# Block-sparse attention and a swish-gated MLP on one core: batch 0 rebuilt with fewer matmuls and another order, and batch 1's values loaded ahead of the last quarter of w_out

## The chip, the cores and the metric

The kernel runs on one core of a Trainium2 chip. The metric is the device time of one execution in microseconds (us). The engines are TensorE (PE; its weight loads are listed apart as PEld), VectorE (DVE), ScalarE (ACT), GpSimd (POOL) and SyncE (SP). Each has a queue of its own that it works off in order. POOL and SP also issue the DMAs: POOL all loads from q, k, v and the weights, SP the copies inside the on-chip memory and the stores.

## What is computed

There are 4 batches, 8 heads, 768 tokens and 64 values per head. Each query sees the keys within 15 positions of its own, and beside them 24 summary keys (the maximum over each block of 32 keys, with log 32 added to the score); the summary values are means over the blocks. The attention's output, 3072 tokens of 512 values, goes through a two-layer MLP with a gate.

```python
mask_l = np.abs(pos[:, None] - pos[None, :]) < window          # window 16
scores_s = scale * np.einsum('bhsd,bhnd->bhsn', q, k_sum) + np.log(block)
scores_all = np.concatenate([np.where(mask_l, scores_l, -1e9), scores_s], axis=-1)
a = softmax(scores_all)
attn_out = a @ np.concatenate([v, v_sum], axis=2)
h = x @ w_in                                                    # 512 -> 2048
g = h * (1.0 / (1.0 + np.exp(-beta * h)))
out = g @ w_out                                                 # 2048 -> 512
```

## The kernel before, in words

The order on every engine is the order in which the program is written (`manual_schedule`); nothing is moved by a scheduler. Heads go in four pairs g = 0 to 3, with the two heads on partitions 0 to 63 and 64 to 127. Batch 0 is worked in an opening stage of its own, in halves `hf` of 384 tokens (3 chunks `m` of 128, each of two parts `par` of 64 queries). Batches 1 to 3 are worked as side work between the matmuls of the MLP (`h_group`, L482, for w_in; `o_part`, L503, for w_out), at places set by the numbers in the last loop (`at_time`).

The opening stage, in the order of the text from L534 on:

- `keep_warm`: eleven matmuls without use, while the first keys (`hold_k`, `hold_q`) arrive. `cast_hold` (L130, on DVE) turns these from f32 into bf16.
- `turn` (L271) transposes k or q of a pair on PE, per pair and tensor 16 matmuls of 64 columns: 8 slices `j` for each of two heads. `prep_k` copies the result to `kw` on ACT, `prep_q` to `qt` on DVE (pair 0: ACT), `top_k` (L285, DVE) takes the block maxima `km`.
- A loop over the pairs. `open_scores` (L354, L355) starts half 0 of a pair with the mask as a matmul: `identity` times `negband` (L354, one per head), and `identity` times `negedge` for the first 16 rows (L355, one per head). `scores_half` adds twelve score matmuls (L367) and two for the summary keys (L372), then Exp on ACT (L386). The loop's order on PE is: open half 0 of g, transpose k of g+1, half 0 of g, transpose q of g+1, half 1 of g. Half 1 of pair 3 is left for later. `band_edges` (DVE, three small instructions that finish the tile `band` for the second halves' mask) stands in the loop's first round.
- `copy_v` copies values to the other alignment (`vo`), half of it on DVE (L320) and half by DMA from SP. `mean_v` makes the block means (`vm_ps`, then `vm_first`, L332). `av_first` (L393 to L401) multiplies attention and values for a first half: one matmul by zeros over all 390 columns (L393), twelve for the near keys, six for the summary keys. `norm` (L446, L447, DVE) divides and gives `x_nat`; `x0` transposes it on PE (L461) and copies it to `xT`. The order is: means of pairs 0 and 1, av_first 0, norm, half 1 of pair 3, `load_beta` (a transpose on PE, L230, and two small DVE instructions, L231 and L232), av_first 1, norm, and so on to pair 3, with the first `h_group` matmuls between them.

POOL's queue is the third order that matters. The program issues, in this row: k and q of batch 0, its values (`load_v_edge`, `load_v`: `ve`, 384 KB per two pairs), w_in in five pieces, k and q of pairs 0 and 1 of batch 1, w_out in four pieces, values of batch 1 (edge and pairs 0 and 1), k and q of pairs 2 and 3, the other values, then batch 2. The framework gives these DMAs eight semaphores in turn, so an issue waits until the one eight places ahead of it has landed. From the landed values SP issues the copies `vo<-ve` of batch 1 (L320), whose landing `rows_v` (L341, DVE) and `av` (L437, PE) wait for.

Of the kernel before, what the change touches and what calls it, by code (L numbers as in the profile page):

```python
# [12 lines left out]
def kernel(  # L13
# [10 lines left out]
    nc = tc.nc  # L24
    ctx.enter_context(tc.manual_schedule(engines={getattr(mybir.EngineType, e) for e in ("SP", "Pool", "PE", "DVE", "Activation")}))
    P = 128
    f32 = mybir.dt.float32
    bf16 = mybir.dt.bfloat16
    ALU = mybir.AluOpType
    ACTF = mybir.ActivationFunctionType  # L30

    B, H, S, D = q.shape
    block = 32
    W = 16
    nb = S // block
    QT = 64
    nch = S // P
    NC = nch + 1
    J = 8
    PT = S // J  # L40
    npair = H // 2
    scale = 1.0 / math.sqrt(D)
# [5 lines left out]
    VW = D + 1  # L48
# [42 lines left out]
    def run_tile(nm, b, g):  # L91
        if (nm, b, g) not in nat:
            t = qk_pool.tile([PT, 4, J, D], bf16, name=nm + "_run", tag=nm + "_nat", bufs=2)
            for i in range(2):
                nat[(nm, b, g // 2 * 2 + i)] = t[:, 2 * i:2 * i + 2]
        return nat[(nm, b, g)]

    def load_run(nm, b, g, n=1):
        src = (k if nm == "k" else q)[b, 2 * g:2 * (g + n)].rearrange("h (p j) d -> p h (j d)", j=J)
        if n == 1:  # L100
            dst = run_tile(nm, b, g)
        else:
            dst = qk_pool.tile([PT, 4, J, D], bf16, name=nm + "_run", tag=nm + "_nat", bufs=2)
            for i in range(n):
                nat[(nm, b, g + i)] = dst[:, 2 * i:2 * i + 2]
        nc.gpsimd.dma_start(out=dst.rearrange("p h j d -> p h (j d)"), in_=src)  # L106
# [7 lines left out]
    def load_v(b, g, n=1):  # L114
        lo, hi = PC * g + 1, min(PC * (g + n) + 1, HC)
        rows = v[b].rearrange("h s d -> (h s) d")
        src = rows[lo * P - W:hi * P - W].rearrange("(c p) d -> p c d", p=P)
        nc.gpsimd.dma_start(out=ve_bufs[b % 2][:, lo:hi, 0:D], in_=src)  # L118
# [7 lines left out]
            nc.gpsimd.dma_start(out=ve[W:P, 0, 0:D], in_=rows[0:P - W])  # L126

    def cast_hold(nm, g, copy):
        f = hold.pop((nm, g))
        copy(out=run_tile(nm, 0, g).rearrange("p h j d -> p h (j d)"), in_=f[:])  # L130

    beta_tmp = wpool.tile([k2, P], f32, name="beta_tmp")
    beta_sb = wpool.tile([P, k2], f32, name="beta_sb")
# [9 lines left out]
    spare = const.tile([P, 1], f32, name="spare")  # L143
    near = const.tile([P, QT], bf16, name="near")
    band = const.tile([P, 2, nch, 2, QT], bf16, name="band")
    negband = const.tile([P, QT], bf16, name="negband")
    negedge = const.tile([P, QT], bf16, name="negedge")
    km_bufs = [const.tile([P, 32], bf16, name=f"km{i}") for i in range(npair)]
    vm_bufs = [const.tile([P, 2, VW], bf16, name=f"vm{i}") for i in range(2)]
    vm_first = const.tile([P, npair, 2, VW], bf16, name="vm_first")  # L150
# [1 line left out]
    def zero(t):  # L152
        nc.vector.memset(t, 0.0)
# [21 lines left out]
    nc.vector.memset(A_loc, 1.0)  # L175
    clear_k(0)
    clear_v(0)
    zero(negedge)
    nc.vector.memset(negedge[0:W], NEG)
    zero(A_avg)  # L180
    load_run("k", 0, 1)
    load_run("q", 0, 1)
# [27 lines left out]
    nc.scalar.copy(out=beta_sb[:, 0:1], in_=warm[:, 0:1])  # L210
    cast_hold("k", 0, nc.vector.tensor_copy)
    cast_hold("q", 0, nc.vector.tensor_copy)
    nc.scalar.activation(out=negband[:], in_=near[:], func=ACTF.Copy, scale=-NEG, bias=NEG)


    for par in range(2):
        nc.scalar.copy(out=band[:, par].rearrange("p m h f -> p (m h) f"), in_=near[:, None].to_broadcast([P, 2 * nch, QT]))

    def band_edges():
        zero(band[0:W, 0, 0])  # L220
        zero(band[D:SUM, 1, nch - 1])
        nc.vector.tensor_copy(out=band[D:D + W, 1, nch - 1], in_=near[D:D + W, None, :].to_broadcast([W, 2, QT]))
# [5 lines left out]
    def load_beta():  # L228
        beta_ps = psum([P, k2], f32, "beta_ps", "big")
        nc.tensor.transpose(beta_ps[:], beta_tmp[:], identity32[:k2, :k2])  # L230
        nc.vector.tensor_copy(out=beta_sb[:], in_=beta_ps[:])  # L231
        nc.vector.reciprocal(out=inv_beta[:], in_=beta_sb[:])  # L232
# [11 lines left out]
    def load_w_out(i, c=k2 // 4):  # L244
        nc.gpsimd.dma_start(out=w_out_sb[:, i * c:(i + 1) * c], in_=w_out_r[:, i * c:(i + 1) * c])
# [19 lines left out]
    def turn(nm, b, g, tag="t"):  # L265

        t = nat.pop((nm, b, g))
        p = psum([P, J, PT], bf16, "p" + nm, tag)
        for j in range(J):
            for h in range(2):  # L270
                nc.tensor.transpose(p[h * D:(h + 1) * D, j], t[:, h, j], identity[:PT, :PT])  # L271
        return p.rearrange("p j t -> p t j")
# [74 lines left out]
    def open_scores(g, hf):  # L347

        big = ps.tile([P, 2, 512], f32, name="s_ps", tag="big", bufs=3)
        s_open[(g, hf)] = big  # L350
        if hf == 0:
            for h in range(2):
                sv = big[:, h, 0:2 * HM * QT].rearrange("p (m r f) -> p m r f", r=2, f=QT)
                nc.tensor.matmul(sv, identity, negband[:, None, None, :].to_broadcast([P, HM, 2, QT]), start=True, stop=False)  # L354
                nc.tensor.matmul(sv[:, 0, 0], identity, negedge, start=False, stop=False)  # L355

    def scores_half(g, hf):
        if (g, hf) not in s_open:
# [29 lines left out]
    def av_first(g, tag):  # L388

        a = at.pop((0, g, 0))  # L390
        o = psum([P, 2 * HM * VW], f32, "av_ps", tag)
        ov = o.rearrange("p (h m e) -> p h m e", h=2, e=VW)
        nc.tensor.matmul(o, warm[:, 0:P], warm[:, 0:2 * HM * VW], start=True, stop=False)  # L393
        for m in range(HM):
            for h in range(2):
                for par, t in ((0, ve_bufs[0]), (1, vo_bufs[0])):
                    nc.tensor.matmul(ov[par * QT:(par + 1) * QT, h, m], a[0:SUM, m, h, par], t[0:SUM, PC * g + nch * h + m],
                                     start=False, stop=False)
        for m in range(HM):
            for h in range(2):  # L400
                nc.tensor.matmul(ov[:, h, m], a[SUM:P, m, h].rearrange("p r f -> p (r f)"), vm_first[SUM:P, g, h],  # L401
                                 start=False, stop=m == HM - 1 and h == 1, tile_position=(SUM, 0))
        ov_of[(0, g, 0)] = ov
# [131 lines left out]
    def x0(g, copy):  # L535
        x_transpose((0, g, 0), 0, HM, "t", copy)
# [8 lines left out]
        load_w_in(i)  # L545
    load_run("k", 1, 0, 2)
    load_run("q", 1, 0, 2)
    for i in range(4):
        load_w_out(i)
    load_v_edge(1, False)  # L550
    load_v(1, 0, 2)
    load_run("k", 1, 2, 2)
    load_run("q", 1, 2, 2)
    load_v(1, 2, 2)
# [2 lines left out]
    for g in range(npair):  # L557
        open_scores(g, 0)
        if g < 3:
            prep_k(0, g + 1)  # L560
        scores_half(g, 0)
        if g < 3:
            prep_q(0, g + 1, copy=dve)
            top_k(0, g + 1)
        if g < 3:
            scores_half(g, 1)
        if g == 0:
            band_edges()
            dve(out=identity32[:], in_=identity[:])
        elif g == 1:  # L570
            fill_avg()

    for g in range(2):
        copy_v(0, g, 0, HM, dve)
        copy_v(0, g, HM, nch)
    mean_v(0, (0, 1), "t", dve)
    av_first(0, "t")
    norm((0, 0, 0), HM)
    scores_half(3, 1)
    load_beta()  # L580
    av_first(1, "big")
    norm((0, 1, 0), HM)
    x0(0, act)
    mean_v(0, (2, 3), "big", act)
    for g in (2, 3):
# [3 lines left out]
    nc.scalar.activation(out=spare[:], in_=warm[:, 0:1], func=ACTF.Silu)  # L589
    av_first(2, "t")  # L590
    norm((0, 2, 0), HM)
    h_group(0, 0, range(2))
    av_first(3, "t")
    norm((0, 3, 0), HM)
    x0(2, act)
    h_group(0, 1, range(2))
    h_group(0, 0, range(2, 3))
    x0(3, act)
    h_group(0, 1, range(2, 3))

    GT, OT = 1.3, 0.865

# [124 lines left out]
```

## Time and profile before

| what | value |
|---|---|
| median of 3 runs (lowest to highest) | 221.83 us (221.42 to 223.22) |
| the profiled execution, its own time | 221.5 us |
| its span from first to last instruction | 219.8 us |
| granted TensorE clock, share of full | 0.998 |
| PE busy | 208.9 us, 95% of the span |
| HBM read and written | 27.27 MB and 6.29 MB |

All places in time below are microseconds from the start of the span. A row of the timeline has start, length, engine, line, operation, output and inputs, shape and count, and in square brackets the idle time of the engine ahead of it with what ended it. Rows of PE overlap: a row's length takes in the way through the array, so the cost of a matmul in a dense row is the distance to the next start. The slices of the page are 40, of 5.5 us each.

### The profile page before, as it was taken

The numbers are of one execution on the slowest core, as the hardware profiler recorded it, in microseconds if no ns is written. First come the engines' busy times: TensorE is split into PE (matmuls) and PEld (weight loads), VectorE is DVE, ScalarE is ACT, GpSimd is POOL, SyncE is SP. The second block draws the span as 40 slices with busy tenths as digits, with TensorE's granted clock in tenths as the row PEclk, the third lists the DMA queues.
The fourth block names the chain that finished last, engine by engine and source line by source line (L and its number), as shares of the span: only waits on it lengthen the run. The fifth ranks groups of instructions, "written<-read, shape, count | busy, mean of one in ns | idle before, by whom it ended". The sixth has DMA issues, their size and how long they took to land.

```text
span 219.8 us, 5132 instructions
## 1 busy us (share of the span) xinstructions
PE 208.9 (95%) x2150; PEld 117.3 (53%) x2168; DVE 93.6 (43%) x239; ACT 118.3 (54%) x162; POOL 60.5 (28%) x81
## 2 busy tenths in 40 slices
PE   7888999999889999999999999999999999999993
PEld 2555556654444556555555456564454466654462
DVE  3688575297587530256645200762444100002121
ACT  5785675778543337667734167668443377740001
POOL 7974334253897001288640000000000000000000
PEclk9999999999999999999999999999999999999999
DMA  6999999999999819999999385780134310001213
GB/s 166 190 147 197 205 206 206 194 183 141 194 173 174 135 48 182 109 181 142 146 172 165 100 158 126 146 87 0 62 89 118 118 49 3 0 0 48 95 59 87
DMA packets 82839, 27.48 MB, mean 125 GB/s; under 512 B 71280, under 2 KB 79488, under 8 KB 82816
## 3 DMA queue, kind: packets, MB, share of 16 engines
q0 software_dynamic: 57072, 13.24, 73.3%
q1 hardware_dynamic: 25360, 13.38, 28.6%
q10 hardware_dynamic: 384, 0.52, 0.9%
q8 instruction: 17, 0.28, 0.6%
q14 instruction: 6, 0.05, 0.1%
HBM read 27.27 MB, written 6.29 MB: 153 GB/s over the span
## 4 chain that ended last, share of the span: by engine, by line
PE 69%; DMA 19%; POOL 6%; DVE 2%; issue 2%; SPq 1%; ACT 0%; POOLq 0%
PE o_ps L503 35%; PE h_ps L482 28%; DMA ve<-in_v_dram 8%; DMA w_in_sb<-in_moe_w_in_dram 7%; DMA vo<-ve 4%; PE av_ps L437 3%; PE s_ps L419 2%; POOL ve L118 1%; POOL w_in_sb L242 1%; POOL q_run L106 1%; SPq L320 1%; POOL k_run L106 1%; PE vm_ps L328 1%; PE px L461 1%; DVE x_nat L447 0%
## 5 line engine op out<-in xcount | busy, mean ns | idle before, releaser
L482 PE MATMUL h_ps<-xT,w_in_sb 128*128 128x384 bf16 x512 | 86.4, 326 | 0.2 <-ACT xT L462 0.2
L503 PE MATMUL o_ps<-w_out_sb,h_sb 128*128 128x512 bf16 (+1 forms) x382 | 84.4, 370 | 2.2 <-issue 1.9
L489 ACT ACTIVATE h_sb<-h_ps,beta_sb 128x768 bf16<-128x768 f32 (+1 forms) x80 | 59.5, 772 | 25.2 <-PE h_ps L482 25.1
L482 PEld LDWEIGHTS <-w_in_sb 128*128 128x128 bf16 x512 | 49.0, 98 | 32.6 <-issue 0.7
L503 PEld LDWEIGHTS <-h_sb 128*128 128x128 bf16 x400 | 37.2, 98 | 39.1
L523 ACT COPY o_sb<-o_ps 128x512 f32<-128x512 f32 x18 | 10.6, 586 | 31.2 <-PE o_ps L503 16.6
L420 ACT ACTIVATE attn<-s_ps 128x768 bf16<-128x768 f32 x24 | 18.1, 808 | 11.6 <-PE s_ps L419 11.6
L424 DVE TENSOR_TENSOR attn<-attn,band 128x768 bf16<-128x768 bf16 x24 | 13.2, 558 | 21.2 <-ACT attn L420 19.8
L118 POOL DMA_DIRECT2D ve<-in_v_dram x12 | 14.3, 1194 | 21.0 <-DVE ve L670 12.3
L523 DVE COPY o_sb<-o_ps 128x512 f32<-128x512 f32 x5 | 3.5, 691 | 38.5 <-PE o_ps L503 38.5
L447 DVE TENSOR_TENSOR x_nat<-av_ps,r 128x768 bf16<-128x768 f32 (+1 forms) x20 | 15.9, 797 | 0.7
L111 POOL DMA_DIRECT2D k_nat<-in_k_dram x16 | 13.5, 846 | 9.9 <-DMA kw<-k_nat 6.8
L303 DVE TENSOR_TENSOR half<-kw 128x384 bf16<-128x384 bf16 x8 | 2.9, 358 | 28.4 <-DMA kw<-k_nat 28.3
L111 POOL DMA_DIRECT2D q_nat<-in_q_dram x16 | 13.3, 833 | 5.5 <-DMA qt<-q_nat 1.7
L516 ACT COPY o_sb<-o_ps 64x256 f32<-64x256 f32 x2 | 0.7, 368 | 19.9 <-DVE o_sb L516 19.9
L285 DVE TENSOR_REDUCE km<-kw 128x24 bf16<-128x768 bf16 x8 | 7.6, 947 | 4.8 <-ACT kw L281 4.7
L446 DVE RECIPROCAL r<-av_ps 128x12 f32<-128x12 f32 (+1 forms) x20 | 4.3, 216 | 11.6 <-PE av_ps L437 10.3
L437 PEld LDWEIGHTS <-attn 128*64 128x64 bf16 x336 | 6.8, 111 | 4.5 <-issue 2.2
L437 PE MATMUL av_ps<-ve,attn 128*64 128x65 bf16 x168 | 8.6, 198 | 0.4 <-DVE ve L341 0.3
L437 PE MATMUL av_ps<-vo,attn 128*64 128x65 bf16 x168 | 8.3, 197 | 0.2 <-DMA vo<-ve 0.2
L386 ACT ACTIVATE attn<-s_ps 128x768 bf16<-128x768 f32 x8 | 6.5, 812 | 2.8 <-PE s_ps L372 2.7
L281 ACT COPY kw<-pk 128x768 bf16<-128x768 bf16 x8 | 6.4, 799 | 2.1 <-PE pk L271 1.9
(90 smaller groups left out, 156.5 us busy)
## 6 DMA issues: line engine op xcount, KB each, us to landing
out_dram<-o_sb SPq DMA_DIRECT2D x23, 256.0 KB, 2.2
w_out_sb<-in_moe_w_out_dram POOLq DMA_DIRECT2D x4, 512.0 KB, 18.7
w_in_sb<-in_moe_w_in_dram POOLq DMA_DIRECT2D x3, 512.0 KB, 13.9
k_nat<-in_k_dram POOLq DMA_DIRECT2D x16, 96.0 KB, 6.8
q_nat<-in_q_dram POOLq DMA_DIRECT2D x16, 96.0 KB, 6.4
vo<-ve SPq DMA_DIRECT2D x12, 97.5 KB, 3.0
ve<-in_v_dram POOLq DMA_DIRECT2D x6, 192.0 KB, 7.5
vo<-ve SPq DMA_DIRECT2D x16, 48.8 KB, 4.8
```

The lines of the kernel that those rows point to most:

```text
L111: nc.gpsimd.dma_start(out=t[:, :, h], in_=(k_row if nm == "k" else q_row)[b, g, :, h])
L118: nc.gpsimd.dma_start(out=ve_bufs[b % 2][:, lo:hi, 0:D], in_=src)
L285: nc.vector.tensor_reduce(out=km_of[g], in_=keys_of(b, g).rearrange("p (n f) -> p n f", f=block), op=ALU.max, axis=mybir.AxisListType.X)
L386: nc.scalar.activation(out=out, in_=src, func=ACTF.Exp, scale=scale)
L420: nc.scalar.activation(out=a.rearrange("p m h f -> p h m f"), in_=sv, func=ACTF.Exp, scale=scale)
L424: nc.vector.tensor_mul(out=a, in0=a, in1=band[:, par])
L437: nc.tensor.matmul(ov[par * QT:(par + 1) * QT, h, m], a[:, par, m, h], t[:, PC * g + nch * h + m0 + m], start=True, stop=True)
L447: nc.vector.tensor_mul(out=x.rearrange("p m h d -> p h m d"), in0=ov[:, :, :, 0:D], in1=r[:, :, :, None].to_broadcast([P, 2, n, D]))
L482: nc.tensor.matmul(big[:, j, 0:MG], w_in_sb[:, ki, ni * P:(ni + 1) * P], xT[b][:, ki, tok:tok + MG], start=(ki == 0), stop=(ki == k1 - 1))
L489: nc.scalar.activation(out=hb.rearrange("p (k m) -> p k m", m=MG), in_=big[:, j:j + w, 0:MG], func=ACTF.Silu, scale=beta_sb[:, ni:ni + 1])
L503: nc.tensor.matmul(o_ps[:, c0:c1], h_bufs[(u, ni * w // k2)][:, ni % (k2 // w), ms * P:(ms + 1) * P], w_out_sb[:, ni, c0:c1], start=(ni == ...
L523: (nc.scalar.copy if u + 1 < len(units) else nc.vector.tensor_copy)(out=o_sb[:], in_=o_ps[:])
```

## The change

1. `turn`, pair 0 of batch 0: the heads are laid side by side by `cast_hold` (the same two casts write in another order), so that 8 transposes of 128 columns per tensor take the place of 16 of 64.
2. The mask: `negband` becomes a whole tile of 128x384 with the edge written into it (by ACT, and one DVE memset), and the `negedge` matmuls (8 in all) and their tile go.
3. `av_first`: the matmul by zeros goes (4 in all); the first matmul of each part starts the sum instead.
4. The loop's order on PE: open half 0 of g, transpose k of g+1, transpose q of g+1, half 0 of g, half 1 of g; half 1 of pair 3 now stands in the loop.
5. `load_beta` moves from behind half 1 of pair 3 to the place right behind the loop, ahead of `copy_v`.
6. `band` is filled by ACT behind the norm of pair 1 in the text (before: at the start), and `band_edges` goes from the loop's first round to the end of the opening stage.
7. `av_first(3)` goes ahead of `h_group(0, 0, range(2))`, and the last two partial h_groups follow x0(3) together.
8. On POOL's queue the values of batch 1, pairs 0 and 1 (edge and `load_v`), go ahead of the last quarter of w_out.

```diff
     def cast_hold(nm, g, copy):
         f = hold.pop((nm, g))
-        copy(out=run_tile(nm, 0, g).rearrange("p h j d -> p h (j d)"), in_=f[:])
+        t = run_tile(nm, 0, g).rearrange("p h j d -> p (h j d)").rearrange("p (j h d) -> p j h d", h=2, d=D)
+        nat[(nm, 0, g)] = t
+        copy(out=t.rearrange("p j h d -> p h j d"), in_=f.rearrange("p h (j d) -> p h j d", d=D))
...
-    negband = const.tile([P, QT], bf16, name="negband")
-    negedge = const.tile([P, QT], bf16, name="negedge")
+    negband = const.tile([P, HM, 2, QT], bf16, name="negband")
...
-    zero(negedge)
-    nc.vector.memset(negedge[0:W], NEG)
...
-    nc.scalar.activation(out=negband[:], in_=near[:], func=ACTF.Copy, scale=-NEG, bias=NEG)
-    for par in range(2):
-        nc.scalar.copy(out=band[:, par].rearrange("p m h f -> p (m h) f"), in_=near[:, None].to_broadcast([P, 2 * nch, QT]))
+    nc.scalar.activation(out=negband.rearrange("p m r f -> p (m r) f"), in_=near[:, None].to_broadcast([P, 2 * HM, QT]),
+                         func=ACTF.Copy, scale=-NEG, bias=NEG)
+    nc.vector.memset(negband[0:W, 0, 0], NEG)
+
+    def fill_band():
+        for par in range(2):
+            nc.scalar.copy(out=band[:, par].rearrange("p m h f -> p (m h) f"), in_=near[:, None].to_broadcast([P, 2 * nch, QT]))
...
         for j in range(J):
+            if b == 0 and g == 0:
+                nc.tensor.transpose(p[:, j], t[:, j].rearrange("p h d -> p (h d)"), identity[:PT, :PT])
+                continue
             for h in range(2):
                 nc.tensor.transpose(p[h * D:(h + 1) * D, j], t[:, h, j], identity[:PT, :PT])
...
-                nc.tensor.matmul(sv, identity, negband[:, None, None, :].to_broadcast([P, HM, 2, QT]), start=True, stop=False)
-                nc.tensor.matmul(sv[:, 0, 0], identity, negedge, start=False, stop=False)
+                nc.tensor.matmul(sv, identity, negband, start=True, stop=False)
...
-        nc.tensor.matmul(o, warm[:, 0:P], warm[:, 0:2 * HM * VW], start=True, stop=False)
...
-                                     start=False, stop=False)
+                                     start=m == 0 and h == 0, stop=False)
...
-    for i in range(4):
+    for i in range(3):
         load_w_out(i)
     load_v_edge(1, False)
     load_v(1, 0, 2)
+    load_w_out(3)
...
         open_scores(g, 0)
         if g < 3:
             prep_k(0, g + 1)
-        scores_half(g, 0)
-        if g < 3:
             prep_q(0, g + 1, copy=dve)
             top_k(0, g + 1)
-        if g < 3:
-            scores_half(g, 1)
+        scores_half(g, 0)
+        scores_half(g, 1)
         if g == 0:
-            band_edges()
             dve(out=identity32[:], in_=identity[:])
...
+    load_beta()
     for g in range(2):
         copy_v(0, g, 0, HM, dve)
...
     norm((0, 0, 0), HM)
-    scores_half(3, 1)
-    load_beta()
     av_first(1, "big")
     norm((0, 1, 0), HM)
+    fill_band()
...
+    av_first(3, "t")
     h_group(0, 0, range(2))
-    av_first(3, "t")
     norm((0, 3, 0), HM)
     x0(2, act)
     h_group(0, 1, range(2))
-    h_group(0, 0, range(2, 3))
     x0(3, act)
-    h_group(0, 1, range(2, 3))
+    for i in range(2):
+        h_group(0, i, range(2, 3))
+    band_edges()
```

Two places of the order, as the built programs have it. The first is DVE's queue behind the loop over the pairs (`vo` are the copied values, `vm_first` the block means, `x_nat` the normed output, `r` its divisor). Before, the two instructions of `load_beta` stand between the first and the second norm:

```order
L332 CAST vm_first<-vm_ps 32x130 x2
L446 RECIPROCAL r_545<-av_ps 128x6
L447 TENSOR_TENSOR x_nat_544<-av_ps,r_545 128x2x3x64
L231 COPY beta_sb<-beta_ps 128x16
L232 RECIPROCAL inv_beta<-beta_sb 128x16
L446 RECIPROCAL r_590<-av_ps 128x6
```

Now they stand right behind the last block maximum, and the copies `vo<-ve` queue behind them:

```order
L291 TENSOR_REDUCE km_114<-kw_88 128x24
L234 COPY beta_sb<-beta_ps 128x16
L235 RECIPROCAL inv_beta<-beta_sb 128x16
L326 COPY vo_83<-ve_81 64x2x195
L326 COPY vo_83<-ve_81 32x2x195
```

What moved: two DVE instructions that wait for PE's transpose of beta now come ahead of the first value copies and no longer behind the first norm.

The second place is POOL's queue around the weights, before (`ve_82` is batch 1's value buffer):

```order
L106 DMA k_run<-in_k_dram 96x4x512
L106 DMA q_run<-in_q_dram 96x4x512
L245 DMA w_out_sb<-in_moe_w_out_dram 128x4x512 x4
L126 DMA ve_82<-in_v_dram 112x64
L118 DMA ve_82<-in_v_dram 128x24x64
```

The same stretch now:

```order
L106 DMA k_run<-in_k_dram 96x4x512
L106 DMA q_run<-in_q_dram 96x4x512
L248 DMA w_out_sb<-in_moe_w_out_dram 128x4x512 x3
L126 DMA ve_82<-in_v_dram 112x64
L118 DMA ve_82<-in_v_dram 128x24x64
L248 DMA w_out_sb<-in_moe_w_out_dram 128x4x512
```

What moved: the fourth quarter of w_out goes behind the two value loads; all issues ahead of and behind these three keep their places.

## The prediction

> **What bounds the kernel now.** I read the page's slices first: the DMA engines are full from the second to the thirteenth, that is from 5.5 to 71.
>
> ```profile
> DMA  6999999999999819999999385780134310001213
> ```
>
> The table of windows splits this (stretch, its length, then busy time and count for PE, PEld, DVE, ACT, POOL, then granted clock, DMA share, GB/s).
>
> ```profile
> 16.50:25.00 8.50, 7.91 (x139) 5.18 (x140) 6.72 (x21) 5.07 (x9) 3.73 (x6) 1.00 1.35 200
> 62.00:219.80 157.80, 152.16 (x1362) 84.14 (x1376) 52.32 (x113) 75.77 (x93) 25.79 (x31) 1.00 0.76 102
> ```
>
> From 62 on PE is busy for 152.16 of 157.80, and the change touches nothing there: whatever is won before 62 stays won. Ahead of it there are two places to price: the opening stage to 26.84, and batch 1's first use of its values near 57. The chain of waits (start, length, what) shows the second: for 30 us it runs through DMAs.
>
> ```profile
> 30.68 17.73 DMA ve<-in_v_dram
> ...
> 50.28 7.77 DMA vo<-ve
> ```
>
> On PE the same place reads so; the last row is DVE's.
>
> ```profile
> 56.83 0.22 PE L437 MATMUL av_ps<-ve,attn 128*64 128x65 bf16 x1
> 57.22 0.19 PE L437 MATMUL av_ps<-vo,attn 128*64 128x65 bf16 x1 [0.17 <-DMA vo<-ve]
> ...
> 57.69 1.04 PE L503 MATMUL o_ps<-w_out_sb,h_sb 128*128 128x512 bf16 x4
> ...
> 61.57 0.51 PE L461 MATMUL px<-identity,x_nat 128*128 128x128 bf16 x6 [0.55 <-DVE x_nat L447]
> ...
> 58.08 0.40 DVE L341 COPY ve<-vm 32x780 bf16<-32x780 bf16 x1 [1.03 <-DMA vo<-ve]
> ```
>
> PE has almost no slack towards these values: it waits a little for them at 57.22, and again at 61.57, because DVE sat 1.03 until the second copy landed at 58.05 and did the norm late. So anything that makes the opening stage shorter would only lengthen these waits, unless the values come sooner. The change does both.
>
> **Part 1, the opening stage.** PE's rows for one round of the loop, with the wait for q at its start:
>
> ```profile
> 6.71 0.53 PE L271 MATMUL pq<-identity,q_run 96*64 96x96 bf16 x16 [0.82 <-DVE q_run L130]
> ...
> 9.69 0.34 PE L354 MATMUL s_ps<-negband,identity 128*128 128x384 bf16 x1
> 9.86 0.19 PE L355 MATMUL s_ps<-negedge,identity 128*128 128x64 bf16 x1
> ...
> 10.17 0.53 PE L271 MATMUL pk<-identity,k_run 96*64 96x96 bf16 x16
> 10.64 0.35 PE L367 MATMUL s_ps<-qt,kw 64*128 64x64 bf16 x12
> 11.12 0.34 PE L372 MATMUL s_ps<-qt,km 64*32 64x384 bf16 x2
> ...
> 12.40 0.34 PE L354 MATMUL s_ps<-negband,identity 128*128 128x384 bf16 x1
> ```
>
> A round takes 12.40 - 9.69 = 2.71. Opening costs 10.17 - 9.69 = 0.48, of which each mask matmul is 0.17; without the two edge matmuls some 0.38 is left, an estimate that keeps one change of kind. The summary matmul at 11.12 comes 0.13 after the end of the scores (10.64 + 0.35); it waits for `km`, and with both transposes ahead of it that wait has cover. So a round becomes about 2.48, and two rounds give 0.46. In the first round q's transpose now stands ahead of the scores and must wait until ACT has emptied q of pair 0, so I count nothing there. Pair 0's 8 transposes for 16 I cost at nothing either: the cast's wait of 0.82 hides them. The cast itself could lose speed with its new order of writing: 0.69 as now, or at most about 1.5, at the rate of DVE's slowest work on f32 (0.56 for 384 values, the row at 24.31 below). I take 0.69, since the runs of 64 values stay whole.
>
> ```profile
> 5.96 0.69 DVE L130 CAST q_run<-hold_q 96x1024 bf16<-96x1024 f32 x1 [0.66 <-DMA hold_q<-in_q_dram]
> ```
>
> What follows the loop on PE:
>
> ```profile
> 16.54 0.34 PE L372 MATMUL s_ps<-qt,km 64*32 64x384 bf16 x2 [0.51 <-DVE km L285]
> ...
> 17.33 0.34 PE L393 MATMUL av_ps<-warm 128*128 128x390 bf16 x1
> 17.59 0.22 PE L397 MATMUL av_ps<-ve,attn 96*64 96x65 bf16 x1
> ...
> 18.49 0.35 PE L367 MATMUL s_ps<-qt,kw 64*128 64x64 bf16 x12
> ...
> 19.03 0.23 PE L230 MATMUL beta_ps<-identity,beta_tmp 16*128 16x16 f32 x1
> ...
> 26.10 0.81 PE L482 MATMUL h_ps<-xT,w_in_sb 128*128 128x384 bf16 x4 [0.24 <-ACT xT L462]
> 26.84 0.22 PE L437 MATMUL av_ps<-ve,attn 128*64 128x65 bf16 x1
> ```
>
> The zero matmul costs 17.59 - 17.33 = 0.26, four of them 1.04. But this stage goes at DVE's pace:
>
> ```profile
> 11.02 0.27 DVE L153 MEMSET band<- 16x64 uint32 x2
> 11.39 0.19 DVE L222 COPY band<-near 16x128 bf16<-16x128 bf16 x1
> ...
> 16.58 1.26 DVE L320 COPY vo<-ve 64x390 bf16<-64x390 bf16 x4
> ...
> 19.30 0.17 DVE L231 COPY beta_sb<-beta_ps 128x16 f32<-128x16 f32 x1
> ...
> 20.17 0.20 DVE L446 RECIPROCAL r<-av_ps 128x6 f32<-128x6 f32 x1 [0.41 <-PE av_ps L401]
> ...
> 20.99 1.58 DVE L320 COPY vo<-ve 64x390 bf16<-64x390 bf16 x4
> ...
> 24.08 0.20 DVE L446 RECIPROCAL r<-av_ps 128x6 f32<-128x6 f32 x1 [0.69 <-PE av_ps L401]
> 24.31 0.56 DVE L447 TENSOR_TENSOR x_nat<-av_ps,r 128x384 bf16<-128x384 f32 x1
> ```
>
> From the first value copy to the last norm it takes 24.87 - 16.58 = 8.29, of which it waits 0.41 + 0.69 = 1.10 for PE's `av_ps`. The first copy cannot come before batch 0's values, issued at 7.3 and landed 9.2 later, at 16.5:
>
> ```profile
> L118 POOL DMA_DIRECT2D ve<-in_v_dram x1: 1452/1452/1452, 7.3 to 7.3; - x1
> ...
> DMA to landing us min/median/max: 9.2/9.2/9.2
> ```
>
> So the shorter loop is partly hidden by that landing. What it does pay for is half 1 of pair 3 (19.03 - 18.49 = 0.54), which now runs before the values are used. And the change adds a wait: the value copies queue on DVE behind beta, beta behind half 1 of pair 3. The loop's last summary matmul comes at 16.54 - 0.46 = 16.1, at best 15.6 if DVE's block maxima keep up (`band_edges`, 0.56 from 11.02 on, no longer stand ahead of two of them). With 0.27 for it, 0.54 for half 1 and 19.30 - 19.03 = 0.27 from beta's transpose to DVE, DVE starts at 16.7 to 17.2. From there the same work without the two waits is 8.29 - 1.10 = 7.19: the last norm ends at 23.9 to 24.4, against 24.87. The waits go because av_first 1 comes 0.54 + 0.17 + 0.26 sooner behind av_first 0 (half 1, beta and the zero matmul are gone from between), and av_first 3 no longer stands behind four h matmuls and a zero matmul. On PE, av_first 3 can run when the second copies are done, at 16.7 + (22.57 - 16.58) - 0.41 = 22.3, and takes about 0.6. Sixteen h matmuls (four in 0.74, 26.10 to 26.84) and two triples of transposes are then left, 3.2, so batch 0's first second-half `av` comes at 26.0 to 26.1 instead of 26.84. DVE's row gives 1.0, PE's 0.8: I take 0.9, between 0.3 (beta at 17.2 and a slower cast, which would push all of this) and 1.3 (beta at 16.6, all waits gone).
>
> The second four copies took 1.58, the first four 1.26, and POOL was issuing w_out beside the second:
>
> ```profile
> 20.70 2.24 POOL L245 DMA_DIRECT2D w_out_sb<-in_moe_w_out_dram  x3
> ```
>
> I keep 1.58, since both keep their places. [...]
>
> Other edits I cost at nothing. The larger `negband` and its memset are done while ACT and DVE wait for the first k and q. `band` on ACT runs behind the last Exp, where ACT has only `xT` to copy, which waits for `x_nat`; without that cover it would hold up pair 0's `xT`, which the first h matmuls need 3 us later. `band_edges` on DVE stands between the last norm and the mask of pair 0's second half, whose `av` PE reaches at 26.0; 23.9 + 0.56 and about 1.1 for mask and summary rows is 25.6. If DVE comes as late as 24.4 it costs 0.1, within my range.
>
> **Part 2, batch 1's values.** The quarter of w_out that they overtake:
>
> ```profile
> 24.86 0.75 POOL L245 DMA_DIRECT2D w_out_sb<-in_moe_w_out_dram  x1 [1.92 <-DMA w_in_sb<-in_moe_w_in_dram]
> ...
> DMA to landing us min/median/max: 19.6/19.6/19.6
> ...
> 50.65 1.65 DVE L235 TENSOR_SCALAR w_out_sb<-w_out_sb,inv_beta 128x512 bf16<-128x512 bf16 x6
> ```
>
> It landed at 44.4, the values at 30.68 + 17.73 = 48.4. POOL's issues come at fixed landings, eight places back, so the three places keep their times and swap their loads. The queue is full and serves in order, so the pair takes the same time: the quarter lands at 48.4, the values one quarter sooner. The price of a quarter is bounded by the gap of landings 48.4 - 44.4 = 4.0 above and nothing below; I take 2.5, half a megabyte at the 200 GB/s of the first window. The same 24 matmuls of `av`, for pair 1, are in the chain of waits without a wait:
>
> ```profile
> 64.94 0.50 PE av_ps L437 x24
> ```
>
> On SP nothing is moved, its four copies wait for the values as before and follow at once, so pair 0's `vo` is there near 54.7 and not 57.2, pair 1's near 55.5 and not 58.05. PE, coming to `av` at 56.83 - 0.9 = 55.9, no longer waits: 57.69 - 56.83 = 0.86 becomes 0.50. The 0.55 at 61.57 goes too, since DVE does the norm up to 2.5 sooner. That is 0.36 + 0.55 = 0.9, between 0.4 (only the first) and 1.2 (if `av` was late as a whole at 56.83 by about as much as within).
>
> Late next: DVE scales the last quarter of w_out as the third of six at 50.65, so at 51.2, now 50.3; it lands at 48.4. That holds by 1.9.
>
> **Sum.** 221.5 (the profiled execution's own time, 1.7 more than its span, 0.33 under the median shown) - 0.9 - 0.9 = **219.7 us**, 0.8% less.
>
> **Rivals.**
> - *More of PE's saving comes through*, DVE keeping up (beta at 16.6): 1.3 + 1.2, 219.0. For it: DVE's waits all name PE. Against: the values' landing at 16.5. Chance 0.25.
> - *The opening stage gains nothing*, as the value copies start behind beta and the rounds stay at 2.71: only part 2 is left, 220.6. For it: DVE is busy 6.72 of 8.50 there. Chance 0.15.
> - *The values do not come sooner* (the loads share the engines and do not land in the order of issue), so part 2 does nothing: PE's gain ends in a longer wait at 57, 221.5, no change. Against: w_out, issued first, landed 4.0 ahead. Chance 0.06.
> - *Slower*: the last quarter of w_out lands after DVE wants it. DVE's queue stands still behind its scaling, with masks and norms, and PE with it. It decides from a landing at 50.3 + 1.8 = 52.1 on; at 53.5, as if the quarter took three times 2.5, it gives 222.9. Against: it would need the fullest queue to halve its rate. Chance 0.04.
>
> **How the numbers follow.** The forecast's case, 219.3 to 220.3, has 0.50. The range 218.7 to 221.0 takes in the two rivals beside it. About 1% (2.2 us, from 221.83 to 219.6) is what a measurement can tell from no change. Faster by over 1%: the first rival's 0.25 and a third of the forecast's case, 0.17, 0.42. Slower by over 1%: 0.03. Within: 0.55.
>
> **What would show it.** Rounds of about 2.5; beta on DVE at 16.7 to 17.2 and no wait of DVE for `av_ps` to the last norm; the first `av` of batch 0's second halves (before at 26.84) near 26.0; values landed near 46, the last quarter of w_out near 48.4; no DMA named ahead of `av` near 56 and no `x_nat` ahead of `px` near 60. It is wrong if a round still takes 2.7, if the copies start after 17.5, or if DVE waits for w_out near 50.

## The result, and the profile after

The changed kernel takes 222.0 us (median of 20 executions, 220.31 to 223.64), the kernel before 221.83 us (20 executions, 221.0 to 224.58). The ratio is 0.9997, with a 95% interval of 0.9977 to 1.0017: no difference. The prediction was 219.7 us, with a range of 218.7 to 221.0.

Ratios here and below leave out executions that lie over 1.5% above the fastest of their kernel; where just these are the point, the executions are listed.

The profiled execution of after, the slowest of its 20 (223.64 us), has a span of 221.3 us and a mean granted clock of 0.977, where before had 0.998. The page's slices (5.5 us each) show where the clock was missing:

```profile
PEclk9699599999999999999999999999999999999999
```

So PE ran at a lower clock in the second and the fifth slice (6 and 5 tenths), both in the opening stage. The table of windows, cut where the clock changes (columns as in the prediction: stretch, length, PE, PEld, DVE, ACT, POOL with counts, granted clock, DMA share, GB/s), first after, then the same place of before:

```profile
14.43:17.85 3.42, 3.35 (x90) 2.14 (x90) 2.35 (x6) 3.07 (x5) 0.94 (x2) 1.00 3.32 146
17.85:21.26 3.41, 2.18 (x53) 1.63 (x52) 2.60 (x10) 2.70 (x4) 1.86 (x3) 1.00 1.25 209
21.26:24.67 3.41, 3.17 (x54) 2.25 (x52) 2.29 (x8) 1.90 (x5) 1.62 (x3) 0.50 1.23 204
24.67:28.09 3.42, 3.42 (x27) 1.97 (x24) 3.06 (x9) 1.53 (x3) 1.09 (x1) 0.50 1.22 204
28.09:31.50 3.41, 3.41 (x35) 2.03 (x34) 1.82 (x6) 2.38 (x5) 1.11 (x2) 1.00 1.24 206
```

```profile
17.71:21.13 3.42, 3.09 (x71) 2.20 (x70) 2.70 (x10) 1.45 (x4) 1.18 (x3) 1.00 1.26 206
```

In this table the clock is 0.50 for exactly two stretches of 3.41 us, and the stretch ahead of them is the one in which PE is busy for 2.18 us and not for 3.09. PE's rows in it (the first three) and behind it:

```profile
18.70 0.22 PE L401 MATMUL av_ps<-ve,attn 96*64 96x65 bf16 x1
19.40 0.19 PE L401 MATMUL av_ps<-vo,attn 96*64 96x65 bf16 x1 [0.47 <-DVE vo L326]
...
20.51 0.34 PE L405 MATMUL av_ps<-vm_first,attn 32*128 32x65 bf16 x6 [0.76 <-DVE vm_first L338]
...
21.73 0.50 PE L465 MATMUL px<-identity,x_nat 128*128 128x128 bf16 x3 [0.24 <-DVE x_nat L451]
...
29.76 0.22 PE L441 MATMUL av_ps<-ve,attn 128*64 128x65 bf16 x1
...
59.41 0.22 PE L441 MATMUL av_ps<-ve,attn 128*64 128x65 bf16 x1
...
63.07 0.50 PE L465 MATMUL px<-identity,x_nat 128*128 128x128 bf16 x6
```

With half 1 of pair 3, beta and the zero matmuls gone from between, PE waits 0.47 + 0.76 = 1.23 for DVE in this stretch, which is all that it lacks of 3.41, and what it does run is small. Then it runs 6.83 us at half clock, and the first `av` of the second halves comes at 29.76, where before had 26.84 and the forecast 26.0. At 59.41 and 63.07 no wait stands, where before had 0.17 and 0.55. That alone does not show part 2 at work: PE comes there 2.6 us later than before, and in experiment 5 these waits are gone without part 2 too. From there to the end all is as it was: 221.3 - 63.07 = 158.2, before 219.8 - 61.57 = 158.2.

The lower clock of the second slice is another halving, from 7.61 to 11.02, behind this stretch:

```profile
4.19:7.61 3.42, 1.54 (x17) 0.87 (x16) 1.69 (x4) 1.03 (x2) 3.42 (x6) 1.00 1.16 190
```

In this execution q came late (its cast starts at 6.68, before at 5.96), and PE stood idle for 1.88 ahead of q's transpose. The second profile of after, in experiment 1, lacks this halving.

In neither stretch ahead of a halving was PE idle throughout: it was busy for 1.54 us of 3.42 ahead of the one in the second slice, and for 2.18 of 3.41 ahead of the later one.

### The profile page after: what moved, and what is told of

It reads as the page before. It is cut to its first block, busy times and chain, and to the rows that moved or that the text cites. A ratio compares the mean times of both kernels' runs of the same rounds, so it can differ in the third digit from the quotient of the medians.

```text
span 221.3 us, 5075 instructions
## 1 busy us (share of the span) xinstructions
PE 210.6 (95%) x2122; PEld 118.6 (54%) x2140; DVE 95.1 (43%) x238; ACT 118.0 (53%) x162; POOL 60.3 (27%) x81
## 4 chain that ended last, share of the span: by engine, by line
PE 92%; DMA 2%; issue 2%; DVE 2%; ACTq 0%; ACT 0%
PE h_ps L486 38%; PE o_ps L507 38%; PE av_ps L441 3%; PE s_ps L423 2%; DMA hold_q<-in_q_dram 2%; PE pk L277 2%; PE px L465 1%; PE pq L277 1%; PE vm_ps L334 1%; PE s_ps L372 1%; PE s_ps L377 1%; PE s_ps L360 1%; DVE vo L326 1%; PE av_ps L405 1%; PE av_ps L401 0%
## 5 line engine op out<-in xcount | busy, mean ns | idle before, releaser
L486 PE MATMUL h_ps<-xT,w_in_sb 128*128 128x384 bf16 x512 | 87.5, 329 | 0.0
L424 ACT ACTIVATE attn<-s_ps 128x768 bf16<-128x768 f32 x24 | 18.1, 808 | 11.1 <-PE s_ps L423 11.0
L423 PEld LDWEIGHTS <-kw 64*128 64x128 bf16 x288 | 4.9, 95 | 4.9 <-issue 4.9
## 6 DMA issues: line engine op xcount, KB each, us to landing
w_out_sb<-in_moe_w_out_dram POOLq DMA_DIRECT2D x4, 512.0 KB, 17.2
```

The costliest lines, as they stand in the source:

```text
L423: nc.tensor.matmul(sv[:, h, m], kw[lo:lo + D, par, m, :], q[lo:lo + D, m, par], start=True, stop=True)
L424: nc.scalar.activation(out=a.rearrange("p m h f -> p h m f"), in_=sv, func=ACTF.Exp, scale=scale)
L486: nc.tensor.matmul(big[:, j, 0:MG], w_in_sb[:, ki, ni * P:(ni + 1) * P], xT[b][:, ki, tok:tok + MG], start=(ki == 0), stop=(ki == k1 - 1))
```

## The experiments

Every version does the whole computation; matmuls added are useless ones, on zeros. Where executions are sorted by clock, "full" is a mean of 0.995 or more.

**1. after_again**: the changed kernel, for more executions.

> The changed kernel once more, unchanged. The profile of it shows PE's clock at half from 7.6 to 11.0 and from 21.3 to 28.1. Theory (the clock: the changed opening stage leaves PE too little work, and its clock is halved): every execution has at least the second stretch, some 6.8 us at half, so a mean granted clock of 0.98 or less, and the ratio to before is 1.00 again. Rival (the queue of DVE: the stage is late because the value copies start behind beta, and the low clock is an accident of one execution): a mean clock of 0.998 as before, and a ratio of 1.00 with the value copies still starting after 18.

222.08 us, ratio 1.0009 (0.9986 to 1.0031). All 10 executions have a clock of 0.975 to 0.985, and the 20 of the first measurement had 0.974 to 0.984, while 22 executions of before beside these have 0.996 to 1.0. The low clock belongs to the change. In this profile it lasts from 18.93 to 29.17, three stretches of 3.41, and so begins elsewhere than in the first profile (21.26).

```profile
PEclk9997589999999999999999999999999999999999
```

**2. values_only**: before with point 8 alone.

```diff
-    for i in range(4):
+    for i in range(3):
         load_w_out(i)
     load_v_edge(1, False)
     load_v(1, 0, 2)
+    load_w_out(3)
```

> The kernel before with point 8 alone: batch 1's values ahead of the last quarter of w_out. Theory (part 2 of the prediction holds by itself; the clock took what it gave): the clock stays near 0.998, no DMA is named ahead of av near 57 and the wait for x_nat near 61.6 goes; 0.4 to 1.2 us less, 0.9 the likeliest, a ratio of 0.996. Rival (values that come sooner are worth nothing, the waits are replaced by others at the same place): ratio 1.000 within 0.001.

220.14 us, 0.9915 (0.9892 to 0.9939), clock 0.997 to 1.0: 1.4 to 2.4 us less, above the forecast. Its PE rows:

```profile
27.22 0.22 PE L437 MATMUL av_ps<-ve,attn 128*64 128x65 bf16 x1
...
56.86 0.22 PE L437 MATMUL av_ps<-ve,attn 128*64 128x65 bf16 x1
...
60.53 0.28 PE L461 MATMUL px<-identity,x_nat 128*128 128x128 bf16 x2
```

From `av` to `px` it takes 60.53 - 56.86 = 3.67, before 61.57 - 56.83 = 4.74: 1.07 for the two waits that I had put at 0.9. From the opening stage's end to `av` it takes 29.64 against 29.99, another 0.35; 0.26 of it is a wait at 32.24 that experiment 6 explains. By the two profiled executions alone the gain is only 221.5 - 220.48 = 1.0, since that of values_only is the slowest of its six and its opening stage ended 0.38 later. One edit of the eight thus wins what the whole change doesn't.

**3. zero_back**: the changed kernel with the zero matmul back.

```diff
+        nc.tensor.matmul(o, warm[:, 0:P], warm[:, 0:2 * HM * VW], start=True, stop=False)
...
-                                     start=m == 0 and h == 0, stop=False)
+                                     start=False, stop=False)
```

> The changed kernel with the four matmuls by zeros put back ahead of av_first (point 3 undone). They cost 0.26 us each on PE at full clock. Theory (the clock): they fill part of the waits for the value copies with 4 x 390 columns of the whole array; if that is enough to keep the clock, the half-rate stretch of 6.8 us goes and the kernel gets faster by 1 to 2 us although it does more; if it isn't enough, the clock is about 0.984 as in after and the time is the same within 0.5 us. Rival (the queue of DVE decides the stage): the matmuls stand in PE's waits or cost up to 1.0 us: same or up to 0.5% slower than after.

A mix of both cases of the theory: the executions fall apart in two groups. Four have a full clock and 218.95 to 219.49 us; seven have 0.974 to 0.985 and 221.57 to 223.01, median 222.68. It is one program and the groups differ in the clock, so I put the difference of their medians, 3.5 us, down to the clock. At full clock the change with four extra matmuls takes 219.2, 0.5 less than the forecast.

**4. fill_gaps**: useless matmuls in PE's waits (`rest` is the unused end of the bank).

```diff
-    def av_first(g, tag):
+    def av_first(g, tag, pre=0, mid=0):
...
+        for _ in range(pre):
+            nc.tensor.matmul(o, warm[:, 0:P], warm[:, 0:2 * HM * VW], start=True, stop=True)
...
+        for _ in range(mid):
+            nc.tensor.matmul(rest, warm[:, 0:P], warm[:, 0:512 - 2 * HM * VW], start=False, stop=False)
...
+    keep_warm(4)
     prep_q(0, 0)
...
-    av_first(0, "t")
+    av_first(0, "t", 3, 14)
...
-    av_first(2, "t")
+    av_first(2, "t", 3)
```

> The changed kernel with useless matmuls (warm, all zeros) put where PE waits: 4 of 512 columns ahead of q's transpose of pair 0, 3 of 390 ahead of av_first 0 and of av_first 2, and 14 of 122 between the near and the summary matmuls of av_first 0. Theory (the clock): the clock stays near 0.998 through 30 us, and what the prediction counted comes through at least in part: 1.0 to 2.2 us less than after, 219.6 to 220.8, a ratio to before of 0.990 to 0.996. Rival (the queue of DVE): the clock may be full, but the first second-half av is still 2 to 3 us late, as in after, and the time is that of after, 222.0.

219.86 us, 0.9902 (0.9878 to 0.9926), all six executions at 0.997 to 1.0: more work, 2.2 us less than after. The rival falls: the first second-half `av` comes at 26.58. DVE now shows the next limit, a wait of 1.24 for beta:

```profile
17.07 0.17 DVE L234 COPY beta_sb<-beta_ps 128x16 f32<-128x16 f32 x1 [1.24 <-PE beta_ps L233]
17.27 0.25 DVE L235 RECIPROCAL inv_beta<-beta_sb 128x16 f32<-128x16 f32 x1
17.56 1.14 DVE L326 COPY vo<-ve 64x390 bf16<-64x390 bf16 x4
...
21.21 1.62 DVE L326 COPY vo<-ve 64x390 bf16<-64x390 bf16 x4
```

**5. part1_only**: the changed kernel with experiment 2's edit undone.

> The changed kernel without point 8: the last quarter of w_out again ahead of batch 1's values (they land near 48.4, their copies near 57 and 58). Theory (the clock; PE comes to batch 1's av 2 to 2.6 us later than before, when the values are there anyway): the time of after, 222.0 within 0.5, mean clock 0.984 or less, and no wait for the values named ahead of av near 59. Rival (part 2's gain, measured as 1.8 on the kernel before, adds to whatever part 1 does): 223.8.

222.27 us, 1.0009 (0.9983 to 1.0035), all ten executions at 0.975 to 0.985. As the theory had it: with the clock halved PE comes to `av` at 57.87, finds the values there, and takes 3.67 from `av` to `px`, as with the values early. Their place no longer matters, and part 2 is worth nothing here.

**6. part1_full_clock**: fill_gaps with experiment 2's edit undone.

> The kernel with the useless matmuls in PE's waits (fill_gaps) without point 8, so part 1 with a full clock and the values as late as before. Theory (the prediction's reading of the kernel before: what the opening stage wins without the values ends in a longer wait near 57): 222.0, that of before, within 0.4, with the wait for vo ahead of av at 56 to 57 longer than the 0.17 of before; against fill_gaps (219.86) it loses about 2. Rival (the opening stage's gain comes through by itself): 221.0 to 221.5.

221.81 us, 0.9991 (0.9973 to 1.0009), clock 0.996 to 1.0 in all ten. PE's rows:

```profile
26.12 0.22 PE L446 MATMUL av_ps<-ve,attn 128*64 128x65 bf16 x1
...
57.42 0.22 PE L446 MATMUL av_ps<-ve,attn 128*64 128x65 bf16 x1 [0.71 <-DVE ve L347]
...
62.11 0.28 PE L470 MATMUL px<-identity,x_nat 128*128 128x128 bf16 x2 [0.61 <-DVE x_nat L456]
```

The opening stage ends at 26.12, within 0.02 of the forecast's 26.0 to 26.1 and 0.72 sooner than before. The prediction has this gain end in the waits at 57 and 62, and these are longer here, by 0.54 and 0.06. But the 0.72 is gone earlier, at a later `av` of batch 0's second halves. The rows there of POOL, DVE and PE, first before, then part1_full_clock:

```profile
30.68 1.45 POOL L118 DMA_DIRECT2D ve<-in_v_dram  x1 [2.43 <-DMA w_in_sb<-in_moe_w_in_dram]
31.76 0.43 DVE L341 COPY ve<-vm_first 32x390 bf16<-32x390 bf16 x1
32.24 0.22 PE L437 MATMUL av_ps<-ve,attn 128*64 128x65 bf16 x1 [0.26 <-DVE ve L341]
```

```profile
30.68 1.45 POOL L118 DMA_DIRECT2D ve<-in_v_dram  x1 [2.25 <-DMA w_in_sb<-in_moe_w_in_dram]
31.04 1.15 DVE L347 COPY ve<-vm_first 32x390 bf16<-32x390 bf16 x1
32.24 0.22 PE L446 MATMUL av_ps<-ve,attn 128*64 128x65 bf16 x1 [0.98 <-DVE ve L347]
```

DVE's copy starts 0.72 sooner and ends at 32.19 all the same, 0.06 after POOL has issued batch 1's values. In the 14 profiles, 30 copies of this shape with no issue of POOL beside them took 0.26 to 0.27. Thirteen took 0.30 to 1.27, and every one of these ended 0.06 to 0.07 after an issue of POOL. Thirteen more had an issue beside them and were not held; what decides that stays open. With point 8 POOL issues the values at 27.0 to 28.2, and PE never waits for this copy. So part 1 needs part 2, as the prediction read it, but first for a wait that it did not price; and the gain of both needs the clock.

**7. no_zero_matmul**: values_only without the zero matmul (point 3 of the change, its two lines of the diff).

> values_only (the kernel before with point 8; 220.1, clock 1.0) with point 3 besides: the four matmuls by zeros gone, all else in its old order. Theory (the clock needs them: they are the densest work of the stretch from 17 to 21): most executions show the half-rate stretch, a mean clock of 0.985 or less and 1 to 3 us more, 221 to 223. Rival (they only cost time: 0.26 each, 1.04 together, of which the queue of DVE leaves 0.3 to 0.8): clock 0.997 or more and 219.3 to 219.9.

Four executions: 219.27 and 219.78 at 0.996 and 0.997, 222.70 and 222.96 at 0.975. Each theory describes half of them: at full clock the four matmuls cost some 0.6 us (220.14 - 219.52, from two executions), and without them the clock is sometimes kept and sometimes lost.

**8. order_back**: the changed kernel with the old order there.

```diff
-        scores_half(g, 1)
+        if g < 3:
+            scores_half(g, 1)
...
-    load_beta()
     for g in range(2):
         copy_v(0, g, 0, HM, dve)
...
     norm((0, 0, 0), HM)
+    scores_half(3, 1)
+    load_beta()
     av_first(1, "big")
```

> The changed kernel with half 1 of pair 3 and beta's transpose back between av_first 0 and av_first 1 (point 5 and the second half of point 4 undone); mask, matmuls by zeros, transposes and the values as changed. Theory A (the order is what thins PE's work out: with half 1 ahead of the values, nothing is left to do while DVE copies them): the clock stays at 0.997 or more in most executions and the time is 219.0 to 219.6. Theory B (the sum of matmuls removed is what counts, the order hardly): half-rate stretches in most executions as in after, 221 to 222.5.

One execution at 1.0, 219.14; three at 0.975 to 0.985, 222.54 to 223.45. Nearer to theory B. Its profile, the stretch ahead of the halving and the low clock that follows:

```profile
13.38:16.79 3.41, 2.27 (x60) 1.28 (x54) 2.31 (x6) 2.33 (x4) 1.37 (x2) 1.00 3.71 142
16.79:27.03 10.24, 10.24 (x136) 6.96 (x134) 7.46 (x25) 6.41 (x11) 4.17 (x6) 0.50 1.32 201
```

Neither the order nor the missing zero matmuls alone are the cause: with either of them undone the clock is still lost in most executions (3 of 4, 7 of 11), where after lost it in all 30.

**9. beta_late**: fill_gaps with beta behind the last norm and fewer useless matmuls.

```diff
-    keep_warm(4)
+    keep_warm(2)
...
-    load_beta()
...
-    av_first(0, "t", 3, 14)
+    av_first(0, "t", 3, 8)
...
     norm((0, 3, 0), HM)
+    load_beta()
```

> fill_gaps (219.9, clock 1.0) with beta's transpose moved from behind the loop to behind the last norm of the first halves, and fewer useless matmuls: 2 for 4 ahead of q's transpose, 8 for 14 ahead of the summary matmuls of av_first 0. In fill_gaps DVE stood 1.24 us waiting for beta_ps (to 17.07) while the values had landed at 16.30. Theory (the queue of DVE sets the stage once the clock is full): the value copies start near 16.4 instead of 17.56, the first second-half av comes about 1 us sooner than the 26.6 of fill_gaps, 218.6 to 219.2 in all, ratio to before 0.985 to 0.988, clock 0.997 or more. Rival (with fewer useless matmuls the clock drops in some executions): times of 221 to 223 among them, with clocks of 0.985 or less.

219.11 us, 0.9874 (0.9854 to 0.9893), clock 0.997 to 1.0, all four executions within 0.24 us: the best version here, 1.3% less than before, and as much under the 222.0 of after. The value copies start when the values land:

```profile
16.45 1.26 DVE L326 COPY vo<-ve 64x390 bf16<-64x390 bf16 x4 [1.14 <-DMA ve<-in_v_dram]
```

```profile
25.73 0.22 PE L446 MATMUL av_ps<-ve,attn 128*64 128x65 bf16 x1
...
59.05 0.22 PE L470 MATMUL px<-identity,x_nat 128*128 128x128 bf16 x1
```

**10. before_again**: another profile of before.

> The kernel before, unchanged, for another profile of it: part 2 alone gave 1.84 us where the first profile of before (own time 221.5) shows waits of 0.36 and 0.55. Theory (the first profile was of an execution with short waits; the landing of the copies vo moves between executions): the waits ahead of av near 57 and ahead of px near 61.6 together are over 0.91, with landings of vo of pair 0 and 1 later than 57.08 and 58.05. Rival (part 2 saves somewhere else as well): the waits are 0.9 again and the own time is near 222.

221.47 us. The profiled execution (221.0) waits 0.88 at `px` and some 0.1 within `av`, 0.98 together:

```profile
61.07 0.23 PE L461 MATMUL px<-identity,x_nat 128*128 128x128 bf16 x1 [0.88 <-DVE x_nat L447]
```

That is hardly over the 0.91 of the first profile, and the second copy landed sooner (DVE goes on at 57.30, there at 58.08), not later. The theory falls, and the own time doesn't fit the rival either. What part 2 wins beyond the waits is not settled by this. One of these eight executions has a clock of 0.975 and 224.06 us, and three of the 73 of before beside the experiments have 0.984 or 0.992: before loses the clock too, but seldom.

**11. fill_thin**: fill_gaps with the useless matmuls of av_first on 32 rows, in another bank.

```diff
-            nc.tensor.matmul(o, warm[:, 0:P], warm[:, 0:2 * HM * VW], start=True, stop=True)
+            nc.tensor.matmul(rest[:, 0:2 * HM * VW], warm[0:32, 0:P], warm[0:32, 0:2 * HM * VW], start=True, stop=True)
...
-            nc.tensor.matmul(rest, warm[:, 0:P], warm[:, 0:512 - 2 * HM * VW], start=False, stop=False)
+            nc.tensor.matmul(rest[:, 0:512 - 2 * HM * VW], warm[0:32, 0:P], warm[0:32, 0:512 - 2 * HM * VW], start=True, stop=True)
```

> fill_gaps with its useless matmuls of av_first 0 and 2 made thin: the same number and columns, but 32 of the array's 128 rows (and into a PSUM bank of their own). PE is as busy by its records. Theory (what counts for the clock is columns times rows in use: in the profiles so far every full-clock stretch of 3.41 us ahead of a halving has 0.49 or less of this, every other 0.54 or more; here it falls to about 0.48): half-rate stretches in most executions, 0.985 or less, and 221 to 223. Rival (what counts is that PE is occupied, whatever part of the array): the clock stays at 0.997 or more and the time at 219.1 to 220.2.

Two of ten executions at full clock (219.44, 219.60), four at 0.988 to 0.992 (220.38 to 221.92), four at 0.973 to 0.976 (223.37 to 224.23). With 128 rows none of six was halved (fill_gaps), nor any of the four of beta_late, measured beside this run; with 32 rows eight of ten. Being occupied isn't enough. The thin matmuls also write another bank, and that was not tried apart. The profiled execution is one of the two at full clock, so how the others lost theirs is not seen; its stretch at 15 us lies just above the theory's 0.49 (0.51, or the 4.19 thousand of the last section):

```profile
14.98:18.39 3.41, 3.26 (x65) 1.99 (x62) 2.08 (x8) 3.22 (x5) 0.82 (x2) 1.00 2.81 161
```

**12. beta_late_bare**: beta_late without any useless matmul.

> beta_late (219.1, clock 1.0 or 0.997 in every execution) without its useless matmuls: the changed kernel with beta's transpose behind the last norm of the first halves and nothing else. Theory (the useless matmuls hold the clock, the place of beta alone doesn't): half-rate stretches in most executions, 0.985 or less, 220.5 to 223; an execution that escapes them shows what the stage would be worth at full clock, 218.4 to 219.1. Rival (with the value copies sooner the waits of PE are short enough by themselves): clock 0.997 or more and 218.4 to 219.1 throughout.

221.52 us, 0.9984 (0.9954 to 1.0014). One execution at 1.0 with 219.05, nine at 0.975 to 0.984 with 220.84 to 222.48. So the useless matmuls hold the clock; the place of beta alone doesn't.

## Why the prediction was wrong, point by point

- **The step that failed** is part 1's subtraction: "The zero matmul costs 17.59 - 17.33 = 0.26, four of them 1.04", and with it half 1 of pair 3, moved out of PE's waits. I took them as cost alone and put what they do for PE's clock at nothing, without a reason; the window that I quoted showed the clock at 1.00, and I did not ask what kept it there. No rival had it. What the runs showed in its place: with them gone PE's clock is halved for 6.8 to 10.2 us, and the opening stage ends at 29.76 and 29.68 in the two profiles of after, not at 26.0 to 26.1. The price, from zero_back's two groups, is 3.5 us. What the edge matmuls of the mask did for the clock was not tried alone.
- **The rounds**: 2.48 forecast. At full clock they take 16.26 - 13.93 = 2.33, opening 0.43 of it where I had 0.38:

```profile
13.93 0.50 PE L360 MATMUL s_ps<-negband,identity 128*128 128x384 bf16 x2
...
16.26 0.50 PE L360 MATMUL s_ps<-negband,identity 128*128 128x384 bf16 x2
16.69 0.60 PE L372 MATMUL s_ps<-qt,kw 64*128 64x64 bf16 x12
```

- **Casts**: kept at 0.69; 0.79 for k and 0.72 for q in after, far from 1.5. Nearly right.

```profile
6.68 0.72 DVE L133 CAST q_run<-hold_q 96x1024 bf16<-96x1024 f32 x1 [1.73 <-DMA hold_q<-in_q_dram]
```

- **Beta on DVE at 16.7 to 17.2**: 18.30 in the profile of after, where half clock had hit the first round too; 16.35 in part1_full_clock and 17.07 in fill_gaps, within 0.4 of the forecast at full clock.
- **DVE's 7.19 from beta's start to the last norm, with no wait for `av_ps`**: 16.35 to 23.90 in part1_full_clock, 7.55, and 17.07 to 24.36 in fill_gaps, 7.29. The ends lie in the forecast's 23.9 to 24.4, but waits of 0.44 and 0.36 for `av_ps` are left, and in part1_full_clock only the early start makes up for it: partly luck. In after it is 18.30 to 26.20, 7.90, with a wait of 0.96 for a PE at half clock.
- **The second value copies, 1.58 beside POOL's issues of w_out**: 1.62 in fill_gaps (at 21.21, w_out issued from 20.51 on), but 1.13 in after, where they ran behind the three issues, which ended at 22.3:

```profile
22.40 1.13 DVE L326 COPY vo<-ve 64x390 bf16<-64x390 bf16 x4
```

  So the four copies took 1.58 and 1.62 with those issues beside them and 1.13 behind them, and the copies of experiment 6 that ended just behind an issue were longer too (0.30 to 1.27 for 0.26). Why, the runs do not show. The first four copies, 1.26 in the prediction's row, had an issue of POOL beside them as well (17.10 to 17.79), so 1.26 is not the time without one.
- **Opening stage to 26.0 to 26.1**: 26.12 in part1_full_clock, 26.58 in fill_gaps and 25.73 in beta_late, so about right at full clock; 2.1 to 3.7 us off with the clock lost (28.14 in part1_only, 29.76 in after).
- **Part 2, landings**: 45.9 for the values and 48.4 for the quarter forecast. In after 27.0 + 17.7 = 44.7 and 30.5 + 16.2 = 46.7, sooner than thought (values first):

```profile
L118 POOL DMA_DIRECT2D ve<-in_v_dram x1: 1446/1446/1446, 27.0 to 27.0; - x1
...
DMA to landing us min/median/max: 17.7/17.7/17.7
```

```profile
L248 POOL DMA_DIRECT2D w_out_sb<-in_moe_w_out_dram x1: 752/752/752, 30.5 to 30.5; - x1
...
DMA to landing us min/median/max: 16.2/16.2/16.2
```

- **Part 2, its worth**: 0.9, between 0.4 and 1.2. Mis-sized: 1.07 between `av` and `px`, 1.42 with the stretch ahead of it, and 1.84 by the medians, with 1.4 the least that the interval allows. The term had two waits only, those at 57 and 62, and left out the one at 32.24. What the medians have beyond 1.42 stays open; a second profile of before showed hardly longer waits.
- **"Whatever is won before 62 stays won"**: from `px` to the end 158.2 in before, after, values_only, fill_gaps and beta_late. Right.
- **The rivals**: in after DVE did not wait for w_out, the values came sooner, and "the opening stage gains nothing" came true for a reason of its own. The sum comes out at full clock (219.2 in zero_back, 219.86 in fill_gaps, 219.7 forecast), but partly by luck: part 2 was worth 1.84 and not 0.9, and part 1 adds 0.3 (fill_gaps) to 0.9 (zero_back) to the 220.14 of values_only.

So the change's 222.0 is a sum of three: part 1 and part 2, to 219 or 220 at full clock, and 2 to 3 us of half clock on top.

## What to carry to other kernels

Before you take matmuls out of a stage in which PE waits for another engine, look at the granted clock there and at how much of the array the rest still uses (fill_thin, with its added matmuls of av_first on 32 of 128 rows, lost the clock in eight of ten executions): a matmul in a wait costs little (fill_gaps, with 24 of them, takes 0.7 us more than zero_back at full clock) and can save 7 to 10 us of half clock behind it. When a change wins nothing, read the row of the clock first, and sort the executions by their mean clock: two groups of the same program, 3.5 us apart, told more here than any median. Try the parts of a change alone: the plainest edit of eight, two loads swapped, was worth 1.84 us by the medians, all by itself.

## What the runs showed of the hardware

Where the tables and slices above show the clock at half, it stays there for one, two or three times 3.41 us (3.41 and 6.83 in after, 10.24 in after_again and order_back), and it was halved though PE was busy for 2.18 us of the 3.41 ahead (after). One count parts the stretches: the columns of every matmul's record times its rows in use, over 128, summed in each stretch of the 14 profiles. Up to 8 us before the end, every stretch at full clock with 4.05 thousand or less (2.9 to 4.05, eight stretches) was followed by half clock, and every one with 4.19 thousand or more was not. Columns alone don't part them (6.1 thousand in a stretch that was followed by half clock, 5.4 in one that wasn't), nor does busy time (2.59 us against 2.44). That fill_thin lost its clock at the same number of columns speaks for the rows. The useless matmuls that held it (0.997 to 1.0 in all executions of fill_gaps and beta_late) multiply nothing but zeros.

It is a count of this kernel's mix, not a law. The gap between 4.05 and 4.19 is small, and some matmul records are missing (382 of 400 for `o_ps` in after). In the last 8 us it fails: a stretch with 2.8 thousand in part1_only and one with 3.6 in after kept the full clock. Nor does it say when the clock returns: in order_back it came back only after three stretches at half, 10.24 us, though PE was busy for all of them, the last with dense `h` matmuls. What gives it back stays open.
